# fp16 attention from the fifth pair of heads on, instead of from the second batch on

## The chip, the cores and the metric

The kernel runs on one core of a Trainium2 chip. The metric is the device time of one execution in microseconds (us), lower is better; the number of a kernel is the median of its runs. The engines are TensorE (PE, with its weight loads PEld), VectorE (DVE), ScalarE (ACT), GpSimd (POOL) and SyncE (SP), whose queue issues nearly all the transfers here.

## What is computed

Attention with normalised q and k over 4 batches of 12 heads (448 positions, head size 64), then two gated feed-forward blocks on the 1792 x 768 result. In numpy, cut to what matters:

```python
q_n, k_n = rmsnorm(q, g_q), rmsnorm(k, g_k)
scores = np.matmul(q_n, k_n.transpose(0, 1, 3, 2)) / 8
attn = np.exp(scores - scores.max(-1)); attn = attn / (attn.sum(-1) + 1e-9)
x = np.matmul(attn, v)            # 4 x 12 x 448 x 64, then reordered to 1792 x 768
x = (x @ w_a) * (x @ w_b) @ w_out             # 768 -> 1536 -> 768
h = x @ w_in                                  # 768 -> 2048
y = (np.maximum(h, 0) + alpha * np.minimum(h, 0)) @ w_out2
```

All weights arrive in a 64-bit float format.

## The kernel before

**Pairs, chunks and steps.** Two heads are worked on as a pair `g`: pairs 0 to 5 are the first batch, 6 to 11 the second, and so on, 24 in all. A pair has seven chunks; a chunk is 64 rows of scores of both heads (128 partitions) against 448 keys. A step `m` of the generator `att_steps` handles two chunks: `scores(m + 1)` on TensorE, `soft(m)` (the maximum on VectorE, L418, and two exponentials on ScalarE, L435) and `probs(m - 1)`. Between them the preparation of later pairs is dropped in (`prep0` to `prep4`), and once all seven chunks of a pair are through, `pv` multiplies the probabilities with v and `pv_out` writes the result `x_0_0` to `x_0_5` as two fp16 halves (L531 on ScalarE, L532 on VectorE).

**Two ways to do a pair.** Pairs of the first batch (`g < NP`, NP is 6) go the fp32 way. q and k are turned by TensorE transposes (L292, L320) and copied back by ScalarE (L303, L309, L321); a chunk's scores are one fp32 matmul; the probabilities are scaled in fp32 (L450 on VectorE), turned by four fp32 TensorE transposes (L455) and copied to the tile `pT` by ScalarE (L463); `pv_f` is eight fp32 matmuls on v as it was loaded. All later pairs go the fp16 way. q and k are scaled on VectorE (L327, L330, L333), split in two fp16 halves (L342, L344 on ScalarE, L350, L353 on VectorE) and turned by transposing transfers (L352, L355), and q's halves are swapped into `qS` by two more transfers (L358, L359); v is split as well (L386, L387); a chunk's scores are four fp16 matmuls; the probabilities are split (L480 on ScalarE, L481 on VectorE) and turned by one transposing transfer a chunk (L487); `pv` is 24 fp16 matmuls. Either way there is one `pT` tile (a pool with one buffer), so the first chunk of the next pair can enter it only after `pv` of the pair before has read it. `pf` has four buffers, `s` (scores in PSUM) two, `p` (PSUM of transposes and of the later matmuls) three, and the split probabilities four.

**The weights.** A weight unit is loaded raw (L629), converted by ScalarE and VectorE (L645, L648, L651), measured (L659), scaled and split in two fp16 halves (L706 on ScalarE, L707 on VectorE) and stored to a scratch in HBM (L710), from which the later batches read it back.

**The order.** The first batch's six pairs run first, with one weight unit pushed forward every second step. Then the stages follow, `a0 y0 h0 o0 a1 y1 a2 h1 o1 y2 a3 h2 y3 o2 h3 o3` (letter: a for w_a and w_b, y for w_out, h for w_in, o for the last; digit: the batch); a table of rates drops steps of the later pairs in between. A unit of stage a0 is 18 matmuls: three for each of the six tiles `x_0_0` to `x_0_5`; a weight is three matmuls per tile because of the halves. A scheduler sets the final order of each engine's queue within this program order, and every engine works its queue strictly in order.

## Time and profile before

| | us |
|---|---|
| median of 3 runs | 1237.91 (1237.06 to 1239.82) |
| the profiled execution | 1242.48 |
| its span, first to last instruction | 1240.7 |
| busy in the span: PE / ACT / DVE | 1169.5 / 740.8 / 679.8 |
| its granted TensorE clock, mean | 0.981 |

The page gives busy shares over the whole span, in which very different stages are mixed: TensorE is busy for 94% of it, ScalarE for 60%, VectorE for 55%. What a change in one stretch does is read from that stretch alone. The attention of the first batch ends with the tile `x_0_5` near 124.6 us, stage a0 ends near 215 us, all conversions of weights are done near 444 us, and from about 560 us on TensorE works nearly without a gap.

### The profile page before, as it was taken

How to read it: one execution, taken by the hardware profiler on the slowest of the kernel's cores; microseconds unless marked ns; L12 is line 12 of the kernel's file. 1: busy time of each engine (PE TensorE's matmuls, PEld its weight loads, DVE VectorE, ACT ScalarE, POOL GpSimd, SP SyncE). 2: the span in 40 equal slices, each digit the busy share in tenths (PEclk: the TensorE clock that was granted, in tenths of full speed). 3: DMA queues.
4: the chain of work that ended last, by engine and by line, in shares of the span. 5: the costliest groups of instructions: out<-in, count | busy, mean ns of one | idle time of the engine just before them, and what ended most of it. 6: DMA issues, size and time to landing. Idle time of an engine off the chain costs nothing.

```text
span 1240.7 us, 18165 instructions
## 1 busy us (share of the span) xinstructions
PE 1169.5 (94%) x6574; PEld 598.9 (48%) x6574; DVE 679.8 (55%) x1455; ACT 740.8 (60%) x1504; POOL 9.2 (1%) x32
## 2 busy tenths in 40 slices
PE   6897998889999799989999999999999999999998
PEld 3553554444444444434455454545555555555554
DVE  7988998979999766677651466332111440102400
ACT  6998999989999966677642465543311441213311
POOL 1000000000000000000000000000000000000000
PEclk9997999897999999999999999999999999999999
DMA  6546999999999999987953737876333333344343
GB/s 185 172 139 184 287 323 306 297 277 306 302 269 300 268 258 243 228 189 183 213 160 115 177 117 164 187 190 164 102 115 115 115 115 110 106 143 131 98 126 90
DMA packets 311242, 234.67 MB, mean 189 GB/s; under 512 B 175440, under 2 KB 284496, under 8 KB 311152
## 3 DMA queue, kind: packets, MB, share of 16 engines
q1 hardware_dynamic: 311040, 233.43, 71.2%
q8 instruction: 52, 0.85, 0.3%
q0 software_dynamic: 112, 0.07, 0.1%
q14 instruction: 38, 0.31, 0.1%
HBM read 155.79 MB, written 32.24 MB: 152 GB/s over the span
## 4 chain that ended last, share of the span: by engine, by line
PE 53%; ACT 1%; DMA 1%; DVE 0%; issue 0%; SPq 0%; ACTq 0%
PE p L108 48%; PE s L108 2%; PE x L108 2%; DMA pT<-p 1%; PE p L884 1%; ACT t L877 0%; ACT pf L435 0%; PE norm L108 0%; ACT p L480 0%; DVE nm L418 0%; SPq L487 0%; DVE p L481 0%; ACT x L531 0%; PE tot L108 0%; DVE v L387 0%
## 5 line engine op out<-in xcount | busy, mean ns | idle before, releaser
L108 PEld LDWEIGHTS <-w 128*128 128x128 f16 x4896 | 475.9, 99 | 473.3 <-issue 45.3
L108 PE MATMUL p<-x,w 128*128 128x448 f16 x1728 | 335.9, 353 | 2.8 <-ACT t L780 2.0
L108 PE MATMUL p<-g,w 128*128 128x448 f16 x1152 | 230.0, 356 | 5.8 <-ACT w L706 2.5
L108 PE MATMUL p<-y,w 128*128 128x448 f16 x1152 | 223.3, 355 | 0.0
L108 PE MATMUL p<-ab,w 128*128 128x448 f16 x864 | 169.6, 356 | 1.7 <-ACT ab L761 1.6
L418 DVE TENSOR_REDUCE nm<-s 128x2 f32<-128x896 f32 x84 | 91.0, 1085 | 38.0 <-PE s L108 37.6
L480 ACT ACTIVATE p<-pf,ri 128x448 f16<-128x448 f32 x126 | 81.8, 663 | 35.3 <-DMA pT<-p 27.6
L108 PE MATMUL s<-kT,qT 128*64 128x448 f16 (+1 forms) x336 | 89.2, 433 | 14.1 <-ACT pf L435 10.3
L481 DVE SCALAR_TENSOR_TENSOR p<-pf,ri,p 128x448 f16<-128x448 f32 x126 | 84.4, 681 | 32.9 <-ACT p L480 32.7
L435 ACT ACTIVATE pf<-s,nm,esc 128x448 f32<-128x448 f32 x126 | 90.0, 718 | 1.3
L859 DVE SCALAR_TENSOR_TENSOR t<-t,al,p 128x448 f32<-128x448 f32 x55 | 37.3, 678 | 95.0 <-ACT t L858 95.0
L783 DVE SCALAR_TENSOR_TENSOR ab<-p,inv_a,t 128x448 f32<-128x448 f32 x48 | 32.6, 678 | 95.5 <-PE p L108 95.4
L707 DVE SCALAR_TENSOR_TENSOR w<-wf,sc,w 128x768 f16<-128x768 f32 (+1 forms) x76 | 70.0, 928 | 5.6 <-ACT w L706 5.3
L877 ACT ACTIVATE t<-p,inv_o 128x448 f32<-128x448 f32 x24 | 25.5, 1063 | 77.3 <-PE p L108 77.3
L645 ACT ACTIVATE wf<-raw 128x768 f32<-128x768 f32 (+1 forms) x76 | 63.1, 831 | 13.0 <-DMA raw<-in_moe_w_in_dram 5.4
L786 ACT ACTIVATE junk<-ab 128x448 bf16<-128x448 f32 x48 | 27.4, 571 | 68.1 <-DVE ab L783 68.0
L651 DVE SCALAR_TENSOR_TENSOR wf<-raw,wf 128x768 int32<-128x768 int32 (+1 forms) x76 | 66.0, 869 | 0.4
L706 ACT ACTIVATE w<-wf,sc 128x768 f16<-128x768 f32 (+1 forms) x76 | 65.0, 863 | 0.7 <-issue 0.7
L659 ACT ACTIVATE junk<-wf 128x768 bf16<-128x768 f32 (+1 forms) x76 | 58.9, 775 | 4.1 <-DVE sc L118 1.2
L858 ACT ACTIVATE t<-p 128x448 f32<-128x448 f32 x55 | 29.8, 541 | 46.8 <-PE p L108 46.4
L844 ACT ACTIVATE g<-t,cgf 128x448 f16<-128x448 f32 x55 | 36.7, 668 | 34.6 <-DVE t L859 34.6
L845 DVE SCALAR_TENSOR_TENSOR g<-t,cgf,g 128x448 f16<-128x448 f32 x55 | 37.5, 682 | 29.5 <-ACT g L844 29.5
(139 smaller groups left out, 1029.1 us busy)
## 6 DMA issues: line engine op xcount, KB each, us to landing
w<-sc_a SPq DMA_DIRECT2D x72, 384.0 KB, 3.1
w<-sc_h SPq DMA_DIRECT2D x48, 384.0 KB, 3.0
w<-sc_o SPq DMA_DIRECT2D x72, 256.0 KB, 3.1
w<-sc_y SPq DMA_DIRECT2D x36, 384.0 KB, 3.1
raw<-in_moe_w_in_dram SPq DMA_DIRECT2D x16, 768.0 KB, 7.3
raw<-in_moe_w_out_dram SPq DMA_DIRECT2D x24, 512.0 KB, 5.5
raw<-in_moe_w_a_dram SPq DMA_DIRECT2D x12, 768.0 KB, 7.0
raw<-in_moe_w_b_dram SPq DMA_DIRECT2D x12, 768.0 KB, 6.5
```

The source lines that it names most:

```text
L108: nc.tensor.matmul(out=o, lhsT=a, rhs=b, start=first, stop=last)
L418: nc.vector.tensor_reduce(out=nm, in_=ps[:, :, 0:S], axis=AX.X, op=ALU.max, negate=True)
L435: nc.scalar.activation(out=pf, in_=ps[:, j, 0:S], func=AF.Exp, bias=nm[:, j:j + 1], scale=scale[j], accum_out=su[:, j:j + 1],)
L480: nc.scalar.activation(out=t[:, 0, :, 0:KP], in_=pf, func=AF.Copy, scale=r)
L481: nc.vector.scalar_tensor_tensor(out=t[:, 1, :, 0:KP], in0=pf, scalar=r, in1=t[:, 0, :, 0:KP], op0=ALU.mult, op1=ALU.subtract,)
L645: nc.scalar.activation(out=t, in_=hi.bitcast(F32), func=AF.Prelu, scale=2.0 ** -112, alpha=-(2.0 ** 32))
L651: nc.vector.scalar_tensor_tensor(out=ti, in0=lo, scalar=29, in1=ti, op0=ALU.logical_shift_right, op1=ALU.bitwise_or)
L659: nc.scalar.activation(out=junk(768, size(kind)), in_=t, func=AF.Square, accum_out=sums[0][:, j:j + 1])
L706: nc.scalar.activation(out=w[:, 0], in_=t, func=AF.Copy, scale=s)
L707: nc.vector.scalar_tensor_tensor(out=w[:, 1], in0=t, scalar=s, in1=w[:, 0], op0=ALU.mult, op1=ALU.subtract)
L845: nc.vector.scalar_tensor_tensor(out=x[:, 1], in0=t, scalar=cgf[:, f:f + 1], in1=x[:, 0], op0=ALU.mult, op1=ALU.subtract,)
L859: nc.vector.scalar_tensor_tensor(out=t, in0=t, scalar=al[:, f:f + 1], in1=ps, op0=ALU.mult, op1=ALU.add)
```

## The change

A constant `FP = 4` takes the place of `NP` (6) wherever the code chooses between the two ways: pairs 4 and 5 of the first batch now go the fp16 way, pairs 0 to 3 stay as they were. The scale of v of the batch (`vscale`) is still found at the same two places, pulled out of the branch. `pv_out` of pairs 4 and 5 scales by a constant, as the scale is in v's halves already. New lines move all later line numbers up by two.

```diff
+    FP = 4
...
-            if g < NP:
+            if g < FP:
                 mm(ps[:, j, 0:S], qT[:, c, :], kT, True, True)
...
-        if 2 * m < NP * NI:
+        if 2 * m < FP * NI:
             for j in range(2):
                 g, c = divmod(2 * m + j, NI)
                 scale[j] = P[g]["r"][:, c:c + 1]
...
     def probs(m):
-        if 2 * m < NP * NI:
+        if 2 * m < FP * NI:
             probs_f(m)
...
     def pv(g):
-        if g < NP:
+        if g < FP:
             pv_f(g)
...
-        s = sx[:, b:b + 1] if b == 0 else 2.0 ** -14
+        s = sx[:, b:b + 1] if g < FP else 2.0 ** -14
...
-                    if g >= NP:
-                        if c == 0 and g % NP == 0:
-                            vscale(g // NP)
+                    if c == 0 and g and g % NP == 0:
+                        vscale(g // NP)
+                    if g >= FP:
                         if c == 5:
                             vprep2(g)
...
-                        (preps_f if g + 1 < NP else preps)[c - 2](g + 1)
+                        (preps_f if g + 1 < FP else preps)[c - 2](g + 1)
```

What moves in the queues is more than these lines say. In the rows below a number behind a name tells one buffer or weight unit from another, and x2 or x8 at the end is a count of equal instructions.

TensorE, before, where the scores of pair 5 (the last fp32 pair) end and those of pair 6 begin:

```order
L108 MATMUL s<-kT_107,qT_1_106 128x448 x2
L455 MATMUL p<-ident,pf 112x128 x8
L108 MATMUL x<-pT,vr 64x448 x8
L455 MATMUL p<-ident,pf 112x128 x4
L108 MATMUL tot<-ss,ones 128x2
L455 MATMUL p<-ident,pf 112x128 x4
L108 MATMUL tot<-ssv,ones 128x6
L455 MATMUL p<-ident,pf 112x128 x5
L108 LDWEIGHTS qT
L108 MATMUL s<-kT,qT 64x448
```

TensorE, after, behind the product with v of pair 4 (`x_4_1307` is its result; w_1097, w_1199 and w_1326 are the first three weight units of stage a0):

```order
L110 MATMUL p<-x_1_727,w_1326 128x448
L110 LDWEIGHTS w_1097
L110 MATMUL p<-x_4_1307,w_1097 128x448
L110 LDWEIGHTS w_1199
L110 MATMUL p<-x_4_1307,w_1199 128x448
L110 LDWEIGHTS w_1326
L110 MATMUL p<-x_1_727,w_1326 128x448
L110 LDWEIGHTS qT
L110 MATMUL s<-kT,qT 64x448
```

The fp32 scores and transposes of pairs 4 and 5 are gone from the queue, and 45 of the 54 matmuls of a0's first three units, all but those of pair 5's tile, stand ahead of the product with v of pair 5. In the kernel before only the first unit has matmuls ahead of that product (six).

VectorE, before, for two chunks of pair 3 (with the half of `x_0_2` in between):

```order
L418 TENSOR_REDUCE nm<-s 128x2
L532 SCALAR_TENSOR_TENSOR x_2_944<-x,sx,x_2_944 128x448
L426 TENSOR_TENSOR nm<-nm,r 128x2
L445 TENSOR_SCALAR su<-su 128x2
L446 RECIPROCAL ri<-su 128x2
L450 TENSOR_SCALAR pf<-pf,ri 128x448 x2
```

VectorE, after, during pairs 4 and 5:

```order
L420 TENSOR_REDUCE nm<-s 128x2
L475 TENSOR_SCALAR su<-su 128x2
L476 RECIPROCAL ri<-su 128x2
L420 TENSOR_REDUCE nm<-s 128x2
L483 SCALAR_TENSOR_TENSOR p_2_111<-pf,ri,p_2_111 128x4x112
L483 SCALAR_TENSOR_TENSOR p_3_112<-pf,ri,p_3_112 128x4x112
L239 TENSOR_REDUCE stat_114<-sk 112x8
L483 SCALAR_TENSOR_TENSOR p_0_109<-pf,ri,p_0_109 128x4x112
```

The scaling of each chunk (L450) has become a split (L483), which also needs ScalarE's half first.

SP's queue, before, up to the first transposing transfers:

```order
L364 DMA vn<-in_v_dram 112x2x256
L217 DMA vr<-in_v_dram 112x2x256
L629 DMA raw<-in_moe_w_b_dram 128x6x128
L352 DMA_TRANSPOSE qT<-q_1238 128x7x128
L355 DMA_TRANSPOSE kT<-k_1240 128x8x112
```

SP's queue, after, from the transfers of pair 6 on (the transfer from p_3_112 is the first chunk of pair 5, the last one before these rows was the last chunk of pair 4):

```order
L357 DMA_TRANSPOSE kT<-k_1232 128x8x112
L354 DMA_TRANSPOSE qT<-q_1230 128x7x128
L489 DMA_TRANSPOSE pT<-p_3_112 128x8x128
L489 DMA_TRANSPOSE pT<-p_0_109 128x8x128
L360 DMA qS<-qT 64x896
L361 DMA qS<-qT 64x896
L489 DMA_TRANSPOSE pT<-p_1_110 128x8x128
L205 DMA kr<-in_k_dram 112x2x256
L209 DMA qr<-in_q_dram 128x448
L712 DMA sc_a_0_564<-w_1326 128x1536
L489 DMA_TRANSPOSE pT<-p_2_111 128x8x128
```

The seven chunks of pair 5 enter `pT` through this one queue, between the transfers of pair 6 and the loads and stores of other work.

## Rows read from the trace of the kernel before

**Rows 1.** Stretches of all engines: length, busy us (instructions) each, PEclk, DMA share, GB/s
```profile
64.00:124.60 60.60, 51.51 (x285) 27.77 (x284) 50.59 (x133) 53.90 (x120) 0.00 (x0) 0.89 0.59 169
82.00:103.00 21.00, 17.22 (x78) 9.14 (x78) 18.66 (x56) 20.64 (x48) 0.00 (x0) 0.92 0.44 146
103.00:124.60 21.60, 16.66 (x83) 8.60 (x80) 16.57 (x36) 16.20 (x34) 0.00 (x0) 0.76 0.90 230
124.60:203.80 79.20, 78.76 (x439) 40.84 (x437) 74.70 (x153) 76.49 (x152) 0.00 (x0) 1.00 1.05 304
203.80:444.00 240.20, 212.21 (x1185) 104.96 (x1185) 207.77 (x436) 216.43 (x437) 1.66 (x5) 0.94 1.10 288
...
560.00:1240.00 680.00, 670.28 (x3712) 343.70 (x3708) 212.16 (x386) 260.59 (x494) 2.18 (x12) 1.00 0.52 138
```

**Rows 2.** TensorE in order of time: start, us, line, tiles, shape, count, [idle before]
```profile
72.51 1.77 PE L108 MATMUL s<-kT,qT 128*128 128x448 f32 x4
74.12 1.04 PE L455 MATMUL p<-ident,pf 128*112 128x128 f32 x8
...
82.03 3.23 PE L108 MATMUL x<-pT,vr 112*64 112x448 f32 x16
...
113.15 0.96 PE L108 MATMUL s<-kT,qT 128*64 128x448 f16 x4 [0.66 <-DMA kT<-k]
...
192.85 3.58 PE L108 MATMUL p<-x,w 128*128 128x448 f16 x18
...
208.78 2.46 PE L108 MATMUL x<-pT,v 112*64 112x448 f16 x24 [1.41 <-DVE tots L131]
```

**Rows 3.** The chain of waits: start, us, what; scores of two chunks, fp16
```profile
578.94 0.88 PE s L108 x8
```

**Rows 4.** VectorE in order of time, columns as for TensorE
```profile
68.09 0.69 DVE L273 TENSOR_TENSOR kd<-kr,r 112x512 f32<-112x512 f32 x1
...
76.39 0.81 DVE L450 TENSOR_SCALAR pf<-pf,ri 128x448 f32<-128x448 f32 x2
...
101.56 0.61 DVE L327 TENSOR_TENSOR qr<-qr,r 128x448 f32<-128x448 f32 x1
102.09 0.68 DVE L333 SCALAR_TENSOR_TENSOR kr<-kr,r 112x512 f32<-112x512 f32 x1
102.69 0.62 DVE L330 TENSOR_TENSOR qr<-qr,gbc 128x448 f32<-128x448 f32 x1
...
104.63 0.62 DVE L350 TENSOR_TENSOR q<-qr,q 128x448 f16<-128x448 f32 x1
105.84 0.69 DVE L353 TENSOR_TENSOR k<-kr,k 112x512 f16<-112x512 f32 x1 [0.59 <-ACT k L344]
...
112.62 0.75 DVE L387 SCALAR_TENSOR_TENSOR v<-vr,sx,v 112x512 f16<-112x512 f32 x1
...
123.96 0.68 DVE L532 SCALAR_TENSOR_TENSOR x<-x,sx,x 128x448 f16<-128x448 f32 x1
125.56 1.27 DVE L481 SCALAR_TENSOR_TENSOR p<-pf,ri,p 128x448 f16<-128x448 f32 x2
```

**Rows 5.** ScalarE in order of time: turning and splitting two chunks
```profile
85.70 1.08 ACT L463 COPY pT<-p 112x512 f32<-112x512 f32 x2
...
124.40 1.23 ACT L480 ACTIVATE p<-pf,ri 128x448 f16<-128x448 f32 x2
```

**Rows 6.** Line 487, whole span: issues on SP (min/median/max ns), and landing
```profile
L487 SPq DMA_TRANSPOSE pT<-p x126: 1231/1314/5493, 126.3 to 861.1; - x126
...
DMA to landing us min/median/max: 3.1/3.9/9.5
```

**Rows 7.** Line 487 from 440 to 460 us, and all engines with and without transposes
```profile
L487 SPq DMA_TRANSPOSE pT<-p x7: 1235/1331/2088, 440.2 to 456.3; - x7
...
440.00:460.00 20.00, 19.71 (x113) 9.49 (x112) 13.84 (x32) 12.91 (x26) 0.00 (x0) 1.00 1.03 243
...
640.00:660.00 20.00, 20.00 (x109) 10.29 (x106) 6.48 (x12) 7.15 (x18) 0.00 (x0) 1.00 0.38 119
```

## The prediction

> **What bounds the kernel now.** I read the busy time by stretches first, since the shares of the whole span hide the stage that the change touches. From 560 us to the end TensorE is busy for 670.28 of 680 us [rows 1]: whatever arrives late at that part comes out late by the same amount. From 203.8 to 444 us no engine is full (TensorE 88%, VectorE 86%, ScalarE 90%), but the transfers are at 1.10, the highest share in these rows [rows 1]; the three engines wait for one another there, and nothing in it is a reserve that could swallow a delay of all of them. So the question is when stage a0 begins and ends. Its pace, from 124.6 to 203.8 us, is TensorE's: 78.76 of 79.2 us busy, while ScalarE has 2.7 us to spare and VectorE 4.5 us [rows 1]. It begins with the second half of `x_0_5`, which VectorE ends at 123.96 + 0.68 = 124.6 us [rows 4].
>
> Before that, from 64 us (where the queues of the two kernels part) to 124.6 us, VectorE is busy for 50.59 of 60.6 us (83%), ScalarE for 53.90 and TensorE for 51.51 [rows 1]. Within it, from 82 to 103 us, ScalarE is full (20.64 of 21) and VectorE at 89%; from 103 to 124.6 us both drop to 16.6 and 16.2 of 21.6 [rows 1]. That hole is the step from the fp32 way to the fp16 way: TensorE gets the turned k of pair 6 only at 113.15 us, behind a transfer [rows 2].
>
> **TensorE.** A pair has seven chunks, so the change touches 14 chunks, or seven times the rows for two chunks. Removed: 7 x 1.77 for scores, 7 x 1.04 for transposes, 2 x 3.23 for the product with v, 26.1 us [rows 2] (the small transposes of q and k go too and are left out). Added: 7 x 0.88 [rows 3] and 2 x 2.46 [rows 2], 11.1 us. So TensorE is relieved of 15 us in a stretch where it isn't what all wait for; by itself that buys nothing. What it does buy is room: a0's first three units now stand in the gaps ahead of `x_0_5`, 45 matmuls, against the 15 that are through in the kernel before when `x_0_5` arrives. A unit of 18 takes 3.58 us [rows 2], so TensorE enters a0 with a lead of 30 / 18 x 3.58 = 6.0 us.
>
> **VectorE.** Added: 7 x 1.27 for the second halves of the probabilities, and per pair the scaling of q and k (0.61 + 0.68 + 0.62), their second halves (0.62 + 0.69) and v's (0.75), 3.97 us: together 8.9 + 7.9 = 16.8 us. Removed: 7 x 0.81 for the scaling of the probabilities and 2 x 0.69 for k: 7.1 us [rows 4]. Net 9.8 us; but neighbouring rows overlap by about 0.08 us (101.56 + 0.61 runs past the next start, 102.09), ten instructions net make 0.8 us of that, so I take 9 us. The 128 x 2 scaling of the maximum moves from VectorE to ScalarE, and is left out of both sums.
>
> **ScalarE.** Two chunks cost 1.23 us of halves instead of 1.08 us of copies [rows 5], 7 x 0.15 = 1 us more. In the preparation two scaled copies and one plain copy per pair give way to two casts and v's first half, three instructions of the same sizes: nothing. ScalarE pays about 1 us, 0 to 3 us with the maxima.
>
> **What that does to `x_0_5`.** VectorE's work up to that tile goes from 50.6 to 59.6 us. At the density of a0 (74.70 of 79.20, 94%) it would need 63 us, 2.6 us longer than now; at the density of the whole stretch now (83%), which has the hole in it, 71.4 us, 10.8 us longer. I take the 89% of 82 to 103 us, since that is the same work at the same place without the hole: 67.1 us, so the same amount of work is reached **6.5 us later**. The hole itself is not a term: it moves from the step between pairs 5 and 6 to the step between pairs 3 and 4, with the same chain (scale, split, turn, swap) in it. Its price is bounded by 5 us of idle VectorE in 103 to 124.6 us [rows 1]: that much comes back if more work of other pairs now covers it, and that much is lost once more if both places show one.
>
> **What a0 gives back.** TensorE starts 6.5 us later with a lead of 6.0 us: it is even. VectorE and ScalarE are 6.5 us late, and now they set the pace. Their reserve in a0, 4.5 and 2.7 us, can be worked off while TensorE doesn't hold them up. I take back 3.5 us, between the two. The end of a0 comes 6.5 - 3.5 = **3 us later**; behind it nothing changes but small reorderings, so 3 us is the sum. The profiled execution took 1242.48 us, 1.8 us more than its span and 0.4% above the median of the runs: 1245.5 us on it, 1237.91 + 3 = **1241 us** on the median.
>
> **The queue of transfers.** 18 transposing transfers are added ahead of a0 (14 of probabilities, four of q and k) and four swaps. An issue holds SP for 1.31 us, and it lands 3.9 us after (3.1 to 9.5) [rows 6]. Since there is one `pT`, pair 5's seven can start only after the product with v of pair 4, then take 7 x 1.31 = 9.2 us, 2.6 us more until the last has landed, and 2.46 us for the product [rows 2]: 14.3 us from product to product, to which the issues between them add a few us. Two pairs take about 2 x 18 us now, so this chain is hidden, but not by much. As to the bandwidth, 440 to 460 us has seven of them and a share of 1.03, 640 to 660 us has none and 0.38 [rows 7]: (1.03 - 0.38) x 20 / 7 = 1.9 us of all 16 engines each, with the loads that go with them. 18 of these in 60.6 us lift the share from 0.59 to 1.12, about the 1.10 that the busiest stretch shows [rows 1]. It just fits; landings will be longer.
>
> On this the Trainium skill speaks against the change: VectorE: DVE Perf Modes, Rules for kernel authors, sends a 128 x 128 transpose to TensorE wherever PSUM will do as a target, and its section on the three transpose paths gives 390 ns there against 1309 ns for a DMA. By that figure a chunk, eight such blocks, would be an estimated 10.5 us by transfer, and the chain of seven 73 us a pair; the trace has a whole chunk landing in 3.9 us [rows 6], so the blocks overlap, and the sum goes by the row.
>
> **Rival 1, the transfers decide (slower, +9 us, 1247).** One `pT`, one queue and a full share: if pair 4's and pair 5's last landings take the 9.5 us seen at worst instead of 3.9 [rows 6], each product with v comes 5.6 us later, and only the first is covered by other work. Then 3 + 5.6 = 8.6 us. For it: the share of 1.12 above, and TensorE's clock, granted at 0.76 on average in 103 to 124.6 us [rows 1], which would run the two products at up to twice 2.46 us. Against it: the median landing of 3.9 us was itself taken mostly in stretches at a share above 1. It decides once product to product takes longer than the engines need for a pair, some 20 us.
>
> **Rival 2, TensorE was the bound and is relieved (faster, -3.4 us, 1234.5).** If VectorE packs its work as in a0, `x_0_5` is 2.6 us late only, TensorE's lead of 6.0 us makes it -3.4 us, and VectorE and ScalarE use up their reserve to follow. For it: a0's 78.76 of 79.2 us, the clearest bound of the whole first half. Against it: ScalarE's reserve is 2.7 us, so it can't follow all the way unless the hole shrinks too, and splits wait for ScalarE's half first, which the old scaling didn't.
>
> **Rival 3, it evens out (0 us, 1238).** The lead, the reserve and the later `x_0_5` cancel, or the transitions between the stages behind a0 swallow the rest.
>
> **How the numbers follow.** Chances: the forecast (+0.5 to +6) 0.42, rival 1 (+5 to +12) 0.20, rival 2 (-1 to -8) 0.24, rival 3 (within 2) 0.14. About 0.2% (2.5 us) is what a measurement of this kernel can tell from no change. The forecast lies on the far side of that for 0.25 of its 0.42, rival 1 wholly: slower 0.45. Rival 2 is faster by more for 0.20: faster 0.21 with a little of rival 3. Same 0.34. Both signs hold much, so the likeliest case alone: 1238.4 to 1244. The range leaves out one in ten at either side: from 1233 (rival 2 with part of the hole gone) to 1249 (rival 1 to +11).
>
> **What would show it.** `x_0_5` ends near 131 us by the forecast, when some probabilities of pair 6 are already split too; past 136 us by rival 1, with ScalarE's L533 waiting for the product and the transfers from 75 to 130 us near 1.1; before 128 us by rival 2. VectorE's density from 82 us to `x_0_5` near 0.9. In a0 TensorE shows gaps of some us (now 0.4) that end on weight halves of ScalarE or VectorE; under rival 2 it has none. From 560 us on both traces are the same, shifted. The forecast is wrong if VectorE stays below 0.85 and the end is still no later, or if a0 takes as long as now from `x_0_5` on although TensorE has its lead.

## The result, and the profile after

| | before | after |
|---|---|---|
| median, us (4 runs each) | 1238.87 | 1254.26 (1251.19 to 1259.16) |
| ratio, 95% interval | 1 | 1.0130 (1.0094 to 1.0165) |
| the profiled execution / its span | 1242.48 / 1240.7 | 1259.16 / 1257.4 |
| busy in the span: PE / ACT / DVE | 1169.5 / 740.8 / 679.8 | 1164.0 / 742.7 / 688.3 |
| granted TensorE clock, mean | 0.981 | 0.963 |

The change makes the kernel 15.4 us slower; the prediction was 1241, with a range from 1233 to 1249. The stretches of after, chosen to answer to [rows 1] (nearly the same lengths behind `x_0_5`, which now ends at 138.20 us instead of 124.6; columns as there):

```profile
64.00:138.20 74.20, 49.41 (x253) 23.53 (x251) 60.39 (x140) 59.83 (x135) 0.00 (x0) 0.73 0.88 207
82.00:103.00 21.00, 13.28 (x80) 6.08 (x77) 18.66 (x39) 17.43 (x42) 0.00 (x0) 0.83 0.96 240
103.00:138.20 35.20, 22.33 (x114) 10.62 (x113) 26.90 (x60) 27.39 (x62) 0.00 (x0) 0.65 1.04 233
138.20:217.40 79.20, 77.14 (x423) 39.07 (x424) 74.67 (x156) 76.44 (x150) 0.00 (x0) 1.00 1.10 324
217.40:457.80 240.40, 208.00 (x1156) 103.16 (x1152) 206.00 (x428) 212.93 (x430) 1.76 (x5) 0.92 1.05 282
577.00:1257.00 680.00, 669.13 (x3697) 342.95 (x3695) 208.63 (x380) 255.69 (x486) 2.11 (x11) 0.99 0.51 137
```

Two things are to be seen. Up to `x_0_5` VectorE has 9.8 us more to do (60.39 instead of 50.59) and takes 13.6 us longer: its density falls from 83% to 81%, where 89% was forecast. And in the 79.2 us behind `x_0_5` VectorE and ScalarE do the same amount as before to 0.05 us (74.67 and 76.44 instead of 74.70 and 76.49): stage a0 started 13.6 us late and caught nothing up. From 577 us on TensorE is as full as it was. So nearly all of the loss is there before a0 ends: 13.6 us at `x_0_5`, 15.1 at the sum of squares that closes a0, 15.4 in the median.

TensorE in order of time (start, us, line, tiles, shape, count, what it waited for): the products with v of pairs 4 and 5, which answer to the 2.46 us of [rows 2], the last matmuls of a0 on the x tiles, a wait for the exponentials, and the sum of squares at the end of a0:

```profile
110.83 4.69 PE L110 MATMUL x<-pT,v 112*64 112x448 f16 x24 [5.77 <-DMA pT<-p]
...
132.27 4.69 PE L110 MATMUL x<-pT,v 112*64 112x448 f16 x24 [2.03 <-issue]
...
219.22 3.20 PE L110 MATMUL p<-x,w 128*128 128x448 f16 x16
...
230.67 0.58 PE L110 MATMUL s<-kT,qT 128*64 128x448 f16 x2 [5.92 <-ACT pf L437]
...
236.12 0.60 PE L110 MATMUL tot<-ssab,ones 128*128 128x12 f32 x2 [3.76 <-ACT junk L788]
```

The same places before, with the first matmuls of the two products and the sum:

```profile
101.22 3.37 PE L108 MATMUL x<-pT,vr 112*64 112x448 f32 x16
...
117.09 1.01 PE L108 MATMUL x<-pT,vr 112*64 112x448 f32 x1
...
221.00 0.60 PE L108 MATMUL tot<-ssab,ones 128*128 128x12 f32 x2 [2.76 <-ACT junk L786]
```

From product to product it is 21.4 us, where it was 15.9. Each product now takes 4.69 us, at the lower of the two clock levels: the granted clock, the third number from the end, was 0.50 during both.

```profile
110.80:115.60 4.80, 4.77 (x25) 2.57 (x25) 4.04 (x7) 3.46 (x10) 0.00 (x0) 0.50 1.35 282
132.20:137.00 4.80, 4.73 (x26) 2.53 (x26) 2.27 (x4) 1.11 (x3) 0.00 (x0) 0.50 0.91 215
```

Pair 5's last two chunks can be followed from engine to engine. VectorE takes their maximum at 105.10; ScalarE gets to the exponentials at 111.30 and to the last split at 123.88; VectorE's half follows, and its transfer stands last of four in SP's queue, which ends at 130.16:

```profile
105.10 1.09 DVE L420 TENSOR_REDUCE nm<-s 128x2 f32<-128x896 f32 x1 [0.33 <-PE s L110]
...
116.14 0.62 DVE L534 SCALAR_TENSOR_TENSOR x<-x,x 128x448 f16<-128x448 f32 x1 [1.30 <-ACT x L533]
...
124.58 0.69 DVE L483 SCALAR_TENSOR_TENSOR p<-pf,ri,p 128x448 f16<-128x448 f32 x1
...
137.58 0.62 DVE L534 SCALAR_TENSOR_TENSOR x<-x,x 128x448 f16<-128x448 f32 x1 [3.11 <-ACT x L533]
```
```profile
111.30 0.73 ACT L437 ACTIVATE pf<-s,nm,esc 128x448 f32<-128x448 f32 x1
...
119.92 0.67 ACT L482 ACTIVATE p<-pf,ri 128x448 f16<-128x448 f32 x1 [1.01 <-DMA pT<-p]
...
123.88 0.67 ACT L482 ACTIVATE p<-pf,ri 128x448 f16<-128x448 f32 x1 [0.37 <-DMA pT<-p]
```
```profile
116.64 2.65 SPq L489 DMA_TRANSPOSE pT<-p  x2
...
123.68 6.48 SPq L489 DMA_TRANSPOSE pT<-p  x4
```

In the fp32 way of before the same maximum was taken at 99.62 us and `x_0_5` was done at 124.6: 25 us. Here it is 33. Before, VectorE's maximum and ScalarE's first exponential behind it:

```profile
99.62 1.09 DVE L418 TENSOR_REDUCE nm<-s 128x2 f32<-128x896 f32 x1 [0.53 <-PE s L108]
```
```profile
101.05 0.80 ACT L435 ACTIVATE pf<-s,nm,r 128x448 f32<-128x448 f32 x1
```

Of these 8 us, 4.8 lie ahead of the exponentials, which begin 6.2 us behind the maximum where it was 1.4.

### The profile page after: what moved, and what is told of

Its sections match the earlier page's. It is cut to its first block, busy times and chain, and to the rows that moved or that the text cites. A ratio compares the mean times of both kernels' runs of the same rounds, so it can differ in the third digit from the quotient of the medians.

```text
span 1257.4 us, 18050 instructions
## 1 busy us (share of the span) xinstructions
PE 1164.0 (93%) x6498; PEld 592.0 (47%) x6498; DVE 688.3 (55%) x1457; ACT 742.7 (59%) x1511; POOL 9.3 (1%) x32
## 4 chain that ended last, share of the span: by engine, by line
PE 52%; ACT 1%; DMA 1%; DVE 1%; issue 0%; SPq 0%; ACTq 0%
PE p L110 48%; PE s L110 2%; PE x L110 2%; DMA pT<-p 1%; PE p L886 1%; ACT t L879 0%; ACT pf L437 0%; DVE nm L420 0%; PE norm L110 0%; ACT p L482 0%; SPq L489 0%; DVE p L483 0%; ACT x L533 0%; PE tot L110 0%; DVE v L389 0%
## 5 line engine op out<-in xcount | busy, mean ns | idle before, releaser
L110 PE MATMUL s<-kT,qT 128*64 128x448 f16 (+1 forms) x336 | 86.4, 432 | 30.8 <-ACT pf L437 22.1
L483 DVE SCALAR_TENSOR_TENSOR p<-pf,ri,p 128x448 f16<-128x448 f32 x140 | 93.6, 680 | 35.8 <-ACT p L482 35.3
L482 ACT ACTIVATE p<-pf,ri 128x448 f16<-128x448 f32 x140 | 90.9, 663 | 35.7 <-DMA pT<-p 22.8
L437 ACT ACTIVATE pf<-s,nm,esc 128x448 f32<-128x448 f32 x140 | 100.1, 719 | 2.0 <-DVE p L483 0.7
L110 PE MATMUL x<-pT,v 112*64 112x448 f16 x480 | 53.7, 377 | 7.8 <-DMA pT<-p 5.8
L110 PE MATMUL s<-kT,qS 128*64 128x448 f16 x280 | 57.0, 383 | 0.7 <-DMA qS<-qT 0.7
```

Of the source, the lines that this page charges most:

```text
L110: nc.tensor.matmul(out=o, lhsT=a, rhs=b, start=first, stop=last)
L437: nc.scalar.activation(out=pf, in_=ps[:, j, 0:S], func=AF.Exp, bias=nm[:, j:j + 1], scale=scale[j], accum_out=su[:, j:j + 1],)
L482: nc.scalar.activation(out=t[:, 0, :, 0:KP], in_=pf, func=AF.Copy, scale=r)
L483: nc.vector.scalar_tensor_tensor(out=t[:, 1, :, 0:KP], in0=pf, scalar=r, in1=t[:, 0, :, 0:KP], op0=ALU.mult, op1=ALU.subtract,)
```

## The experiments

All times are of each kernel's profiled execution, in us: the start of the maximum of pair 5's last two chunks, the start of the product with v of pair 5, the end of `x_0_5`, and a0's sum of squares. The ratio is against runs of before on the same chip (medians 1238.87 to 1242.58), with its 95% interval.

| kernel | last max | product | `x_0_5` | a0's sum | ratio |
|---|---|---|---|---|---|
| before | 99.6 | 117.1 | 124.6 | 221.0 | 1 |
| after | 105.1 | 132.3 | 138.2 | 236.1 | 1.0130 (1.0094 to 1.0165) |
| e1_scores16 | 106.8 | 121.0 | 126.8 | 223.2 | 1.0067 (1.0045 to 1.0088) |
| e2_probs16 | 103.6 | 133.7 | 139.7 | 238.2 | 1.0138 (1.0104 to 1.0173) |
| e3_two_pT | 104.1 | 128.8 | 134.2 | 232.9 | 1.0118 (1.0095 to 1.0140) |
| e4_half_turn | 103.4 | 128.0 | 134.8 | 233.1 | 1.0151 (1.0115 to 1.0187) |
| f1b_turn_order | 106.4 | 128.8 | 136.7 | 238.5 | 1.0118 (1.0089 to 1.0146) |
| e5_scores_x4 | 110.7 | 132.9 | 138.9 | 241.0 | 1.0167 (1.0143 to 1.0191) |
| d3_late_pv | 104.2 | 131.3 | 140.3 | 240.9 | 1.0225 (1.0200 to 1.0250) |
| s1_pool | 120.0 | 141.7 | 147.1 | 242.4 | 1.0258 (1.0207 to 1.0309) |
| s2_pool_two_pT | 122.6 | 143.9 | 149.6 | 245.1 | 1.0242 (1.0211 to 1.0273) |
| d4_short_square | 102.6 | 129.8 | 135.7 | 235.1 | 1.0141 (1.0117 to 1.0165) |
| n1_after_null | 105.7 | 132.4 | 138.3 | 239.6 | 1.0139 (1.0105 to 1.0173) |
| n0_before_null | 99.2 | 113.5 | 119.5 | 217.3 | 0.9996 (0.9977 to 1.0014) |
| d1_dve | 104.6 | 119.8 | 128.0 | 224.3 | 1.0144 (1.0123 to 1.0166) |
| d2_dma | 99.5 | 114.1 | 121.2 | 231.1 | 1.0092 (1.0069 to 1.0115) |
| d12_both | 104.1 | 120.0 | 125.8 | 226.7 | 1.0104 (1.0078 to 1.0131) |
| h3_one_hop | 101.0 | 118.3 | 125.9 | 222.5 | 1.0007 (0.9989 to 1.0024) |
| h1_hops | 101.4 | 117.5 | 124.7 | 229.1 | 1.0077 (1.0047 to 1.0107) |
| h2_hops_loads | 102.9 | 120.5 | 126.2 | 233.0 | 1.0121 (1.0083 to 1.0160) |

**Which part of the change.** One constant became two: FS for the preparation of q and k and the scores, FP for the probabilities and v.

```diff
-    FP = 4
+    FS, FP = 4, 6    # e1; e2 has 6, 4
```

> Only the scores of pairs 4 and 5 go the fp16 way (scaled and split q and k, turned by four transposing transfers, swapped); their probabilities and products with v stay fp32 and on TensorE. Theory A (the turned probabilities travel through one queue into one pT, and that chain makes x_0_5 late): nearly none of the 15 us, 0 to +4 us on the kernel before, since no probability is transferred. Theory B (the added work of VectorE makes it late, 9 us of it in the full change): 5 of the 9 us of VectorE are here (per pair 0.61 + 0.68 + 0.62 + 0.62 + 0.69 added, 0.69 removed), so some 8 of the 15 us.

> The other part alone: scores of pairs 4 and 5 fp32, probabilities split and turned by 14 transposing transfers, v split, product with v in fp16. Theory A: most of the loss, +10 to +15 us. Theory B: VectorE has 8.9 + 1.5 - 5.7 = 4.7 us more here, so about half, +7 to +8 us, and the two parts add up to the whole.

By the medians the probabilities alone cost what the whole change costs, and the scores alone half (the eight runs of e1 lie from 1243.5 to 1245.4 and from 1248.2 to 1251.7 us, and the profiled one is in the first group). The parts don't add. The column to read is the way from the last maximum to `x_0_5`: 20.0 us in e1 and 36.1 in e2, 25.0 before and 33.1 after. Every kernel with fp16 probabilities in pair 5 takes 27 to 36 us there, every kernel without 20 to 25. The late exponentials aren't what separates the two: in e1 they begin 5.5 us behind the maximum, and `x_0_5` is 2.2 us late.

**What makes that way long.** Four parts of it were taken away one at a time. A second place for pair 5's turned probabilities (in the room of the fp32 q and k):

```diff
-  P[g]["pT"] = one_p.tile([128, 2 * KB, NI, 128], F16, tag="pT", name="pT")
+  P[g]["pT"] = pT1 if g == 5 else one_p.tile([128, 2 * KB, NI, 128], F16, tag="pT", name="pT")
```

> The changed kernel, with a second place for the turned probabilities of pair 5 (the room of the fp32 q, k tiles, which are done by then), so that its seven transfers need not wait for the product with v of pair 4. Theory A with the one buffer as its cause: the 21 us from product to product fall to the 15 to 16 us that they take in the kernel before, 4 to 7 us off the changed kernel, +8 to +11 us on the kernel before. Theory A with landing and share of the transfers as its cause, or theory B: within 2 us of the changed kernel.

Half of the bytes (only the first halves are turned for pairs 4 and 5, and only they are multiplied, 16 matmuls instead of 24, which the cut doesn't show):

```diff
-  nc.sync.dma_start_transpose(out=P[g]["pT"][:, :, c, :], in_=...)
+  nc.sync.dma_start_transpose(out=P[g]["pT"][:, 0:KB, c, :], in_=...)   # 4 <= g < 6
```

> The changed kernel, but of the probabilities of pairs 4 and 5 only the first fp16 half is turned and used: the second half is still computed by VectorE and then left out (14 transfers of half the size, 16 instead of 24 matmuls a product). Theory A: issue and landing of each are shorter, 5 us or more off the changed kernel. Theory B: VectorE's work is the same, within 2 us of the changed kernel.

They bring `x_0_5` forward by 4.0 and 3.4 us, and neither makes the kernel faster than after. Next the order of SP's queue, on top of e3 (pair 6's first scores also go a step later, which the cut doesn't show):

```diff
+    with tc.issue_after(tr[5].ins):    # tr[5]: the last transfer of pair 5's probabilities
+        prep4(6)
```

> The kernel e3_two_pT (after, with a second place for pair 5's turned probabilities), with the turning and swapping transfers of pair 6's q and k placed behind pair 5's last transfer of probabilities in SyncE's queue, and pair 6's first scores a step later; no work is added or left out. In e3 pair 5's splits were done at 119.6, but their last two transfers were issued at 124.2 to 126.8, behind pair 6's turns and swaps, and the product began at 128.8. (Q) if the order in SyncE's queue makes the tail of pair 5, the product starts at 122 to 126 and x_0_5 is done at 126 to 131 (134.2 in e3). (R) if the tail is the length of split, landing and product at the low clock, x_0_5 stays within 2 us of 134. In both cases pair 6 is later by some us, so the time may stay at 1250 to 1256.

The queue's order did change, but the product begins at 128.8 us as in e3 (2.3 us less behind the last maximum), and from the last maximum to `x_0_5` it is 30.3 us, as long as in e3 (30.1): TensorE takes pair 6's scores in the middle of the product, which lasts until 135.24 us. What stood behind pair 6's turns in e3 now waits for its own split, VectorE's last at 121.48:

```profile
120.81 0.68 DVE L483 SCALAR_TENSOR_TENSOR p<-pf,ri,p 128x448 f16<-128x448 f32 x1
...
121.48 0.67 DVE L483 SCALAR_TENSOR_TENSOR p<-pf,ri,p 128x448 f16<-128x448 f32 x1
```
```profile
116.11 5.49 SPq L489 DMA_TRANSPOSE U<-p  x2
...
123.30 3.05 SPq L489 DMA_TRANSPOSE U<-p  x2
126.44 1.25 SPq L354 DMA_TRANSPOSE qT<-q  x1
```

So this change of SP's order doesn't shorten the way by itself either. The clock:

```diff
+            for _ in range(4 if g < NP else 1):
                 for l in range(2):
                     for h in range(2):
                         mm(ps[64 * h:64 * h + 64, j, 0:S], ..., l == 0, l == 1)
```

> The kernel after, with the fp16 scores of pairs 4 and 5 computed four times over, which keeps TensorE at work there (some 0.88 x 3 us more per two chunks, 18 us in all, in a stretch where it is idle for more). In after the products with v of pairs 4 and 5 took 4.69 us each at the lower clock, 2.46 at the higher. (C) if the lower clock is a part of x_0_5's lateness, the products take about 2.5 us, x_0_5 is 2 to 5 us earlier than 138.2 and the time is 1249 to 1252. (N) else x_0_5 is within 2 us of 138 or later, time 1253 to 1259.

This one is inconclusive. It held the clock at 1.00 from 84 to 104 us, but pair 5's product still took 4.69 us (pair 4's 4.02), and the longer scores made the last maximum 5.6 us later:

```profile
132.94 4.69 PE L110 MATMUL x<-pT,v 112*64 112x448 f16 x24 [0.48 <-issue]
```

Two attempts to give the queues something else to do made it worse. Putting the product and its `x` a step later on top of e3 made everything later, and the time worse than either theory said:

```diff
-  if done < B * NP and 2 * (m - 1) >= (done + 1) * NI:
+  if done < B * NP and 2 * (m - (2 if FP <= done < NP else 1)) >= (done + 1) * NI:
```

> The kernel after with a second place for the turned probabilities (as in e3_two_pT, 1254.5, x_0_5 done 134.2), and with the products with v of pairs 4 and 5 and their two halves of x put one step (two chunks) later in the program, so that ScalarE's and VectorE's queues have work to do while the last transfers land. (R) round trip: x_0_4 no longer holds up the queues, both engines' waits of 3 to 6 us on x go, x_0_5 itself is some 1 to 4 us earlier than in e3 although asked for later (130 to 134), total of a0 near 228 to 231, time 1247 to 1251. (V) and (T): the engines' work is what counts and the order only postpones x_0_5, by up to 4 us: x_0_5 135 to 138, time 1255 to 1258; but if ScalarE's work and not x_0_5 sets a0's end, the total stays near 233.

And issuing the plain transfers of that stretch from GpSimd's queue (`dq()` gives it in place of `nc.sync`), without and with e3's second place:

```diff
-        nc.sync.dma_start(out=qS[0:64], in_=qT[64:128])
+        dq().dma_start(out=qS[0:64], in_=qT[64:128])
```

> The kernel after, with the plain transfers of the stretch from about 65 us to x_0_5 (loads of q, k, v and raw weights, stores of the split weights, the swaps of q's halves) issued by GpSimd's queue, which is idle, instead of SyncE's, so that SyncE issues little but transposing transfers there. (Q) if SyncE's queue, full for 17.9 of 18.3 us ahead of pair 5's last issue, holds the product with v of pair 5, it starts 3 to 6 us earlier than 132.3 and x_0_5 is done at 132 to 135; the product of pair 4 moves by 0 to 2 us from 110.8. (R) if it is the length of the round trip as such (split, landing, product at the low clock), x_0_5 stays within 2 us of 138.

> As s1_pool, with a second place for the turned probabilities of pair 5 as well (e3_two_pT, x_0_5 done 134.2, 1254.5). (Q) queue and place add up: product of pair 5 at 122 to 126, x_0_5 done at 128 to 131, time 1244 to 1250 if the later order doesn't spoil it. (R) x_0_5 at 133 to 135 as in e3_two_pT.

Both are far slower, so they don't test the queue: SP's own transposing issues became long instead. Here are those of pair 5's q and k and of three chunks in s1_pool, against 1.23 us for q and 3.23 us for k after (single issues of up to 5.49 us occur in before too [rows 6]):

```profile
80.09 5.36 SPq L357 DMA_TRANSPOSE qT<-q  x1
85.55 6.93 SPq L360 DMA_TRANSPOSE kT<-k  x1
92.57 13.66 SPq L492 DMA_TRANSPOSE pT<-p  x3
```

**Added work that nobody reads.** Now the other side: the kernel before, with VectorE's fourteen halves alone, with fourteen transposing transfers alone (each behind a copy of 8 columns), and with both, as the cut shows. The results go to places of the fp16 q and are read by nobody.

```diff
             nc.vector.tensor_scalar(pf, pf, ri[:, j:j + 1], None, op0=ALU.mult)
+            if g >= 4:
+                t = p16[(2 * m + j) % len(p16)]
+                nc.vector.scalar_tensor_tensor(out=t[:, 1, :, 0:KP], in0=..., op0=ALU.mult, op1=ALU.subtract)
+                d = two_p.tile([128, NI, 128], F16, tag=n, name=n)
+                nc.sync.dma_start_transpose(out=d, in_=...)
```

> The kernel before, all fp32 in the first batch, with nothing added but VectorE's fourteen fp16 lower halves for the chunks of pairs 4 and 5 (a scalar_tensor_tensor per chunk, some 0.68 us each, 9.5 us in all); nobody reads them, so no transfer, no change of the products. Three theories for the 13.6 us by which the second half of x_0_5 came later (138.2 instead of 124.6): (V) VectorE's added work is the cause by itself: x_0_5 done near 134 to 138, first total of the squares of a0 near 231 to 235 (221.0 before), time near 1250. (R) the round trip at each pair's end is the cause (last split, issue, landing some 6 us later, product at the low clock, while ScalarE and VectorE stand behind x): VectorE's work alone hides in its idle time but for a part, x_0_5 127 to 130, time 1241 to 1244. (T) the transfers as such: x_0_5 125 to 127, time 1239 to 1241.

> The kernel before, with nothing added but fourteen transposing transfers of 128 x 896 fp16 in pairs 4 and 5 (one per chunk, seven blocks instead of the change's eight, from the four split buffers into the places of the fp16 q), each tied to its chunk by a VectorE copy of 8 columns; nobody reads the results. (T) if the load on SyncE's queue and on the transfer engines is the cause, x_0_5 is done near 134 to 138 and the time near 1250. (R) the transfers cost only where somebody waits for them at a pair's end: x_0_5 125 to 128, time 1239 to 1242. (V) the same as R here.

> The kernel before with VectorE's fourteen halves (as in d1_dve) and fourteen transposing transfers of them, seven blocks each (as in d2_dma), in pairs 4 and 5; nobody reads the results. Each alone left x_0_5 at 128.0 and 121.2 (124.6 before). (R) if the loads only hurt where somebody waits for them, x_0_5 is done by 131. (L) if the two loads together, on VectorE and on SyncE's queue, make the lateness, 134 to 138.

None of the three makes `x_0_5` late by more than 3.4 us. With both loads VectorE simply packs its work: 20.60 of 21 us, where it had 18.66 before [rows 1] and after.

```profile
82.00:103.00 21.00, 15.78 (x68) 8.39 (x64) 20.60 (x57) 20.88 (x47) 0.00 (x0) 0.92 0.96 229
```

So it isn't the amount of VectorE's work and of the transfers that makes `x_0_5` late. What is left is the waiting on the way (ScalarE's added work wasn't tried alone). But the loads cost 12 to 18 us at the end all the same, and with that tile nearly on time, which no theory had said. In the trace of d12_both a0's sum is 5.7 us late with `x_0_5` only 1.2 us late; in d2_dma it is 10.1 us late although `x_0_5` came 3.4 us early. In d1_dve the sum is 3.3 us late, the norm of the first batch's y comes 2.3 us early (278.44), and a1's sum is 14.3 us late (571.68): its loss lies between those two, where nothing was added. Nor does the cost follow the amount: VectorE's halves alone cost 18.4 us, and with the transfers on top 13.3.

Part of what the transfers cost can be read from the traces. Nobody reads their results, but other transfers stand behind them in SP's queue. Here is the eleventh load of raw weights in before, d12_both and after, and ScalarE's wait for one in d12_both:

```profile
119.26 0.48 SPq L629 DMA_DIRECT2D raw<-in_moe_w_a_dram  x1
```
```profile
127.83 0.57 SPq L640 DMA_DIRECT2D raw<-in_moe_w_a_dram  x1
```
```profile
135.36 0.59 SPq L631 DMA_DIRECT2D raw<-in_moe_w_a_dram  x1
```
```profile
133.22 0.90 ACT L656 ACTIVATE wf<-raw 128x768 f32<-128x768 f32 x1 [3.35 <-DMA raw<-in_moe_w_a_dram]
```

In d12_both five of the added transfers, 6.9 us of issue, stand ahead of it between 115.81 and 126.16 us. So the weights of a0 come later, by 8.6 us in d12_both, where `x_0_5` is nearly on time, and by 16.1 in after. How much of the loss that makes stays open: s1_pool and s2_pool_two_pT took these loads off SP's queue, but don't test it, as said.

Since every edit also reorders the queues, two controls add fourteen copies of 8 columns (0.16 us each in n0's trace, 2.0 us in all, more than was expected):

> A control: the kernel before with fourteen VectorE copies of 8 columns (some 0.06 us each, under 1 us in all) in pairs 4 and 5, which nobody reads. They cost nothing, but the scheduler may put the queues in another order. In the run with VectorE's halves alone (d1_dve) the tile x_0_5 was 3.4 us late, the end of the first feed-forward product (the sum ahead of y0's norm) 2.2 us early, and still the end was 18 us late: the loss came between 444 and 706 us, where no work was added. (O) if that is the doing of the queues' order, this control moves too, by 3 us or more in either direction, with a lag that does not arise in 60 to 125 us. (W) if it is the work, the time stays within 2.5 us of before.

> The same control on the kernel after: fourteen VectorE copies of 8 columns in pairs 4 and 5. x_0_5 within 2 us of the 138.2 of after. (O) the end moves by 3 us or more against after (1254.3), by the order of the later stages. (W) within 2.5 us of after.

On before the time doesn't move, though `x_0_5` came 5.1 us earlier in the trace; on after it is 2.3 us further from before than after was, with overlapping intervals. A shuffle of the order alone is thus worth 1 to 3 us in these two, not 15.

**Lateness without work.** Last, the kernel before with `x_0_5` alone made late, by copies on GpSimd's queue:

```diff
+        if g == 5:
+            for i in range(3):               # h3: range(1)
+                y = slot(f"hop{i}")
+                nc.gpsimd.dma_start(out=y, in_=X[b, p])
+                X[b, p] = y
```

> The kernel before, with x_0_5 copied on by three transfers one behind the other, on GpSimd's queue, before stage a0 may use it: x_0_5 alone comes later, by some 9 to 12 us (three issues and landings of some 3 to 4 us), while every engine's queue and work stay as they were. (X) if it is x_0_5's lateness that comes out at the end, a0's sum of squares is 8 to 12 us later than 221.0 and the end 8 to 14 us later. (E) if a0 and what follows go by the work of ScalarE, VectorE and the transfers on the weights, and x_0_5's lateness in the other runs only showed that these queues had stood still, the sum comes at most 4 us later and the end within 4 us of before.

> The kernel before with x_0_5 copied on once by a transfer before a0 may use it, on GpSimd's queue: x_0_5 is usable some 5 us later than 124.6 (three hops: some 15 us, a0's sum +8.1, time +9.8). (X) if lateness comes out in proportion, the sum is 2 to 4 us later and the time +2 to +5. (G) if a0 takes back the first 5 to 7 us and passes the rest on, the sum and the time stay within 1.5 us of before.

```profile
125.00 0.56 POOL L539 DMA_DIRECT2D hop<-x  x1 [115.67 <-DVE x L532]
128.70 0.54 POOL L539 DMA_DIRECT2D hop<-hop  x1 [3.15 <-DMA hop<-x]
133.31 0.54 POOL L539 DMA_DIRECT2D hop<-hop  x1 [4.07 <-DMA hop<-hop]
```
```profile
140.09 3.52 PE L108 MATMUL p<-hop,w 128*128 128x448 f16 x9 [7.23 <-DMA hop<-hop]
```
```profile
124.60:144.60 20.00, 12.77 (x64) 6.10 (x63) 10.90 (x25) 10.74 (x23) 1.63 (x3) 0.77 0.87 225
```

One hop, some 4 us (TensorE gets the tile at 128.77), is swallowed: 1.0007. Three hops, some 15 us until TensorE gets the tile, come out as 8.1 us at a0's sum and 9.8 us in the median; VectorE and ScalarE stand still for half of those 20 us (10.90 and 10.74 busy). So a0 gives about half back when nothing else is added. ScalarE's work by itself does not set a0's pace: with its squares of the weights cut to 8 columns,

```diff
+        n_sq = 8 if kind == "a" else size(kind)
-            out=junk(768, size(kind)), in_=t, func=AF.Square, accum_out=sums[0][:, j:j + 1]
+            out=junk(768, n_sq), in_=t[:, 0:n_sq], func=AF.Square, accum_out=sums[0][:, j:j + 1]
```

> The kernel after with ScalarE's squares of the weights of stage a (about 24 of 0.7 to 0.8 us, of which some 20 lie before the end of a0) taken over 8 columns instead of 768; what is left out is the rest of the sum of squares, so the scales are not the reference's. It tells what sets a0's end after x_0_5 (96.4 us from x_0_5 to the total before, 97.9 after). (S) ScalarE, 95 of 100 busy there, sets the pace: some 0.6 us per unit are saved, the total comes 8 to 15 us earlier (221 to 228 instead of 236.1), the time falls to 1240 to 1246. (P) TensorE or the products set it: the total stays within 3 us of 236 less what x_0_5 itself gains, time 1251 to 1255.

the 79.2 us behind `x_0_5` hold 8 us less of ScalarE's work (68.06 instead of 76.44) and the same of VectorE's, and a0 takes as long as in after (99.4 us from `x_0_5` to the sum, 97.9 there):

```profile
135.70:214.90 79.20, 77.71 (x427) 39.18 (x427) 74.64 (x156) 68.06 (x149) 0.00 (x0) 1.00 1.10 319
```

The two halves together, d12_both's loads and h1_hops' three copies in the kernel before:

> The kernel before with both things put in together that were put in apart: VectorE's fourteen halves and fourteen transposing transfers that nobody waits for (d12_both, +13.3 us in the median, +9.9 in the trace, x_0_5 at 125.8), and x_0_5 copied on three times before a0 may use it (h1_hops, +9.8 in the median, +11 in the trace). (A) if after's loss is the sum of these two, work that is added and a tile that comes late, they add up here for the most part: the time is +15 to +23 us, 1256 to 1264, a0's sum of squares 12 to 16 us later than 221.0, like in after (+15.1). (M) if the engines' stand-still while a0 waits for x_0_5 is used up by the added work, the larger of the two alone shows: +9 to +14, 1250 to 1255.

| lag behind before, us | a0's sum (221.0) | norm of the first batch's y (280.7) | a1's sum (557.4) | a2's sum (706.5) | a3's sum (969.3) |
|---|---|---|---|---|---|
| h1_hops | 8.1 | 6.6 | 7.1 | 8.7 | 11.0 |
| d12_both | 5.7 | 3.6 | 6.6 | 8.3 | 9.9 |
| h2_hops_loads | 12.0 | 10.4 | 12.9 | 14.1 | 15.5 |
| after | 15.1 | 11.7 | 12.8 | 14.4 | 16.7 |

From the norm on the kernel with both lies within 1.3 us of after at every mark, and its median is 14.6 us above before (after: 15.4). Up to 557 us the two parts add to within 2 us; at a3's sum 15.5 is less than their 20.9, and the medians (9.8 and 13.3) add even less. This is one trace of each, and the match is partly luck: the runs of this kernel spread over 7.6 us, and its tile reaches TensorE 6 us later than in after, where the first matmul on `x_0_5` is at 137.60:

```profile
143.63 3.19 PE L108 MATMUL p<-hop,w 128*128 128x448 f16 x9 [4.08 <-DMA hop<-hop]
```

Nor do the medians say that both are needed: 1.0121 with the late tile and 1.0104 without it (d12_both) have overlapping intervals. What they show is that either way of disturbing a0 costs most of the loss by itself, and that both together cost about what the change does.

## Why the prediction was wrong

The sum was 6.5 us at `x_0_5` less 3.5 us given back in a0. Measured were 13.6 us at `x_0_5`, where the chain of the transposing transfers had been set to nothing, and 1.5 us more, instead of 3.5 less, at a0's sum. These two terms are 12.1 of the 12.4 us between 3 and 15.4.

**TensorE: right, and worth nothing.** The last matmuls of a0 on the x tiles ended at 219.22 + 3.20 = 222.4 us, before at 211.17 + 3.58 = 214.75, so 7.7 us later with an `x_0_5` 13.6 us later: a lead of 5.9 us, where 6.0 was worked out. But the sum at a0's end waits for ScalarE (5.92 and 3.76 us of idle TensorE at 230.67 and 236.12), and that is 15.1 us late. The row of before:

```profile
211.17 3.58 PE L108 MATMUL p<-x,w 128*128 128x448 f16 x18
```

**VectorE: the work right, its price wrong.** 9.8 us more were measured up to `x_0_5`, 9 forecast. Turning them into 6.5 us of lateness by a density of 89% failed: where nobody waits for them they cost 3.4 us there (d1_dve) or, with the transfers, 1.2 (d12_both). ScalarE has 5.9 us more in that stretch, where about 1 and up to 3 with the maxima was forecast; 2.3 of it are the scalings of the maxima (L433, ten instead of two), and a part is other work that came into the longer stretch.

**"This chain is hidden, but not by much": the step that failed first.** It was weighed from product to product, 14.3 us plus issues against 18 us a pair, and set to nothing. It was 21.4 us. What the sum left out, besides the lower clock (4.69 us for the product instead of 2.46), is that every chunk now changes engine more often: exponential, reciprocal, ScalarE's half, VectorE's half, SP's issue and landing in place of VectorE's scaling, TensorE's transposes and one copy. Each change of engine means joining the end of a queue that is worked in order and that itself waits for the product of the pair before (1.30 us of VectorE ahead of 116.14) or a free split buffer (1.01 us of ScalarE at 119.92). That this sum of small waits, and no single one, makes the way long is what is left after e3 and e4 took away one each and got 3 to 4 us at `x_0_5`, and f1b none on top of e3; it wasn't shown by taking all away, and more split buffers weren't tried.

The hole moved as told, and at its new place it is larger than its bound of 5 us: the first maximum of pair 4 is at 83.89 instead of 74.32 us, 9.6 us late.

```profile
74.32 1.09 DVE L418 TENSOR_REDUCE nm<-s 128x2 f32<-128x896 f32 x1 [1.01 <-PE s L108]
```
```profile
83.89 2.09 DVE L420 TENSOR_REDUCE nm<-s 128x2 f32<-128x896 f32 x2 [1.51 <-PE s L110]
```

But the hole by itself is caught up. e1 has it too and e2 hasn't, as the first maximum of pair 4 shows in them, and behind it the second half of `x_0_4` in e1, e2 and before (116.14 us in after, above):

```profile
83.67 2.09 DVE L420 TENSOR_REDUCE nm<-s 128x2 f32<-128x896 f32 x2 [1.60 <-PE s L110]
...
110.62 0.68 DVE L534 SCALAR_TENSOR_TENSOR x<-x,sx,x 128x448 f16<-128x448 f32 x1 [2.17 <-ACT x L533]
```
```profile
77.06 1.09 DVE L420 TENSOR_REDUCE nm<-s 128x2 f32<-128x896 f32 x1 [1.00 <-PE s L110]
...
116.31 0.62 DVE L534 SCALAR_TENSOR_TENSOR x<-x,x 128x448 f16<-128x448 f32 x1 [5.34 <-ACT x L533]
```
```profile
107.35 0.68 DVE L532 SCALAR_TENSOR_TENSOR x<-x,sx,x 128x448 f16<-128x448 f32 x1
```

With the scores alone, hole included, `x_0_4` is 3.3 us late and `x_0_5` 2.2. With the probabilities alone they are 9.0 and 15.1 us late, with both 8.8 and 13.6. So the way of the probabilities makes the lateness, and it does so in pair 4 already; the 5.6 us more from product to product are only pair 5's part.

**What a0 gives back: 3.5 us forecast, nothing measured.** A late `x_0_5` alone is forgiven its first 4 us (h3_one_hop), and 7 of 15 (h1_hops), so the size was possible. After forgave nothing and lost 1.5 us more. The added loads alone don't explain that: with them and a tile some 19 us late (143.63) the sum came 12.0 us late (h2_hops_loads), so 7 us were given back there too. The row nearest to a reason is the load of raw weights at 135.36, 16.1 us late in after and 8.2 in h2_hops_loads (127.44), but no run tested it.

**The term that was missing** is one for work that is added ahead of a0 and costs something behind `x_0_5`. The sum counted VectorE's and the transfers' load only as far as they move that tile. With the tile nearly on time they cost 13.3 us (d12_both). Up to 444 us all engines and transfers are near full [rows 1], and the prediction said itself that "nothing in it is a reserve that could swallow a delay of all of them", but it priced only the tile's delay. What such work costs per us isn't shown, since VectorE's part alone cost more than both. Why d1_dve's loss comes only behind the first batch's norm stays open, and so does what sets a0's pace: the transfers, at 1.05 of their time there before and 1.10 after, weren't varied.

**Rival 1** named the sign and the marks: `x_0_5` past 136 us, ScalarE's L533 waiting (3.11 us passed on to L534 at 137.58), transfers at 1.04 of their time in the last 35 us (0.99 from 75 to 130 us, near 1.1 forecast). Its condition was met too, 21.4 us from product to product where it said some 20. Its lever was wrong: landings did not grow, the fourteen of pairs 4 and 5 took 3.1, 3.3 and 6.1 us (least, median, most) against 3.1, 3.9 and 9.5 in [rows 6]:

```profile
DMA to landing us min/median/max: 3.1/3.3/6.1
```

The estimate of the share was too high as well: 18 transfers of 1.9 us on top of 0.59 come to 1.14 or 1.15 and not 1.12, and the share measured from 64 us to `x_0_5` was 0.88. The Trainium skill (VectorE: DVE Perf Modes, Rules for kernel authors) sends a 128 x 128 transpose to TensorE where PSUM will do as a target. The ratios of e1, whose probabilities are turned on TensorE (1.0067), and e2, where transfers turn them (1.0138), point the same way, but the two differ in more than that, so they don't test the rule alone. Rivals 2 and 3 fell with `x_0_5` at 138.

## What to carry to other kernels

Where a step goes from one engine and one copy to a chain over four in-order queues, look at how long the last chunk of a group takes to come through the whole chain, where nothing else covers it, and not only at the throughput of the longest link. In a stretch where several engines are above 85%, work isn't free because nobody reads its result: look at what stands behind it in the same queue. Here it cost 12 to 18 us, and not in proportion to its amount. A tile can be made late alone, with copies on an idle queue, and work can be added alone, with results that nobody reads. Together they cost nearly what the change costs, but their single prices don't add, so neither is its share of the loss.

## What the runs showed of the hardware

A transposing transfer held SP's queue for 1.23 us at best, and a chunk of eight 128 x 128 blocks landed in 3.3 us in the median. While GpSimd's queue issued plain transfers, single transposing ones held SP's queue for 5.36 and 6.93 us, and moving transfers to that idle queue made the kernel 13 to 15 us slower still. The 24 matmuls of the product with v took 4.69 us at a granted clock of 0.50 and 2.46 us [rows 2] at 1.00 (before, 208.70 to 211.20 us), 2.2 us more a pair; ahead of the two products in after TensorE had been idle for 5.77 and 2.03 us.
